# Eight places for x in the column loop, and VectorE's product rooms moved to the transform's input

## The chip, the cores and the metric

One core of a Trainium2 chip runs the whole program. The metric is the device time of one execution in microseconds (us); lower is better. The engines are called as in the profile: PE (TensorE, with PEld its weight loads), DVE (VectorE), ACT (ScalarE), POOL (GpSimd) and SP (SyncE, which here only issues DMA transfers).

## What is computed

A long convolution gated by its input, and then a small expert layer on 128 rows of each of four batches. Cut to what matters:

```python
# x, v: (4, 12608, 128); pos_emb: (12608, 64)
h = np.maximum(pos_emb @ w1, 0.0) @ w2 * np.exp(-0.01 * pos)[:, None]
y = irfft(rfft(x * v, n=2 * S) * rfft(h, n=2 * S))[:, :S]
out = x * y                                   # the gated convolution
scores = out @ moe_w_gate                     # one number per row
top = 128 rows of each batch with the highest scores
out[top] += sigmoid(scores[top]) * (np.maximum(out[top] @ moe_w1, 0) @ moe_w2)
```

## The kernel before, in words

After a filter stage (up to about 106 us) the program goes through 4 batches of 32 groups, a group being 4 of the 128 channels. One group per iteration `t` of the main loop (L1079) passes through a pipeline: transfers of x and v (`load_u`, L253) and their product on POOL (`stage_u`, L259), first transform stage on PE (`f_s1`, L436) with ACT's copy into `te` (L438), second stage on PE (`dft`, L278) with ACT's copy into `qs` (L281), butterflies and the product with the filter on DVE (L445, L442, L450, L451, L456, L457), two sums on POOL (L463, L464), and three iterations later the inverse stage on PE (`f_i`, L273) with ACT's copies into `big` (L487, L488). PE takes the matmuls in the order in which the program is written, and so does every other engine.

When the last group of a batch has gone through `f_i`, the column loop (`P1.run`, L618) runs for that batch, before the next iteration of the main loop. It has 32 half blocks `h` of 4 columns; two half blocks make a block, 16 blocks in the order `ORD`. For a half block PE makes 4 columns (L553, L557), DVE multiplies them in place by x (`fin`, L568), DVE or, for some, POOL multiplies the result by the gate's weights into a room of 4 x 128 numbers (`weigh`, L602), and ACT sums the four columns of that room (L612). DVE's rooms are used in turn, four of them (L621); a room comes free when ACT's sums have read it. From `h` = 28 (`NL`) on, other rooms are used and the sums are left for later, but not in the last batch. After the second half block of a block SP stores it (L591) and fetches the x of a block that comes later (`load_a`, L530).

A block's x lies in a place of 8 x 128 numbers, and seven places are used in turn: block number i of the order lies in place i % 7. Five are their own (`xa`), and two (`XE`) lie over buffers that are free during the loop: the first over `qs` and the start of `mt` (DVE's L450 writes `mt`), the second over `ws` and the start of `yz` (DVE's L456 writes `yz`). The first five blocks of a batch are fetched in halves, one half in each of the ten iterations of `LA` (L44, L1140 to L1144); the two in the XE places when the loop starts; the other nine in the loop. When block i has been multiplied, SP is given the store of block i and behind it the fetch of block i + 6 into the place of block i - 1, which waits until the store of block i - 1 has landed. SP works in order, so everything behind that fetch waits with it.

After the loop the next iteration follows, and its first ACT copy into `qs` (L281) waits until the store from the XE place over `qs` has landed. At the start, iterations t = 0 to 2 fill the five places with zeros on ACT (L1097, L1098).

Of the kernel before, what the change touches and what calls it, by code (L numbers as in the profile page):

```python
# [23 lines left out]
NG = 32  # L24
HC = 4 * N1
# [4 lines left out]
HB = 4  # L30
# [10 lines left out]
PJ = (N3 + 1) // 2  # L41
NC, CO = 4, 2
NE = 3
LA = range(32 - 12, 32 - 2)  # L44
NS, ND = 66, 4
NWARM = 8
JB = 9
# [5 lines left out]
DW = (2, 14)  # L53
OFF, _o = {}, 0
for _n, _k, _w in (("te", 2, 2 * HC), ("qs", 2, HC), ("mt", 1, 2 * HC), ("ws", 1, 888), ("yz", 2, 2 * HC), ("sd", 2, 2 * HC),
                   ("ht", NH, 2 * HC), ("xa", NX, 8 * D), ("wx", 2, HB * D), ("cm", 2, 2 * NC * D), ("x", NU, XC), ("", 1, 2), ("v", NV, XC)):
    OFF[_n] = (_o, _k, _w)
    _o += _k * _w
ARENA = _o
XE = [OFF["qs"][0] + k * 12 * D for k in range(2)]  # L60
CE = [o + 8 * D for o in XE]
POS0, HID0 = 0, PJ * N1


# [107 lines left out]
def hyena_moe(ctx, tc, xg, x2, pos, bw, ww, wg, mw1, mw2, fo, fc, c1, gx, cf, ci, wm, tk, out):  # L172
# [18 lines left out]
    def buf(name, k, shape):  # L191
        o, n, w = OFF[name]
        return view(arena, o + (k + (name == "yz")) % n * w, shape)
# [11 lines left out]
        return view(bank2[k], 0, shape)  # L205

    def gap(k, n):
        return bank2[k].rearrange("p (c x) -> p c x", c=2)[:, :, HC:HC + n]

    def c3(a):  # L210
        return a.rearrange("p (c x) -> p c x", c=2)
# [300 lines left out]
    class P1:  # L512
# [10 lines left out]
        def load_a(self, i, a=0, z=8):  # L523
            if i < len(ORD):
                k = ORD[i]
                j0, j1 = blocks[k]
                z = min(z, j1 - j0)
                o = i % (NX + len(XE))
                self.xa[k] = buf("xa", o, [128, 8, D]) if o < NX else view(arena, XE[o - NX], [128, 8, D])
                nc.sync.dma_start(self.xa[k][P0:P0 + PR, a:z], x2[self.b, :, j0 + a:j0 + z])  # L530

        def comb(self):
# [27 lines left out]
        def fin(self, h):  # L560
            ja, n = self.hbs[h]
            blk = ja // 8
            xa = self.xa[blk]
            js = slice(ja % 8, ja % 8 + n)
            end = self.last and h >= len(self.hbs) - 2
            if end:
                self.weigh()
            nc.vector.tensor_tensor(out=xa[:, js], in0=self.s4.pop(h)[:, :n], in1=xa[:, js], op=ALU.mult)  # L568
            if not end:
                self.weigh()  # L570
                far = ja >= JM and h + 1 < len(self.hbs) and h not in DW
                if h >= NL and not self.last:
                    o = OFF["cm"][0] + 2 * NC * D if h < 30 else OFF["wx"][0]
                    wx = view(arena, o + h % 2 * HB * D, [128, HB, D])
                elif far:
                    wx = view(arena, CE[self.pw % 2], [128, HB, D])
                    self.pw += 1
                else:
                    wx = view(arena, self.wx[self.nw % 4], [128, HB, D])
                    self.nw += 1  # L580
                self.mul = xa[:, js], wx[:, :n], ja, n, far, h
                if far:
                    self.weigh()
            else:
                for k in range(n):
                    nc.vector.scalar_tensor_tensor(out=junk, in0=xa[:, ja % 8 + k], scalar=1.0,
                                                   in1=self.wg, op0=ALU.mult, op1=ALU.mult,
                                                   accum_out=self.sc[:, ja + k:ja + k + 1])
            if ja + n == blocks[blk][1]:
                j0, j1 = blocks[blk]  # L590
                nc.sync.dma_start(out[self.b, :, j0:j1], xa[P0:P0 + PR, :j1 - j0])  # L591
                i = ORD.index(blk)
                if i:
                    self.load_a(i - 1 + NX + len(XE))
                if blk in CB:
                    self.comb()

# [20 lines left out]
        def run(self, ex):  # L618
            self.last = ex is not None
            self.ring = (0, 1, 2) if ex else (3, 2, 0, 1)  # L620
            self.wx = [OFF["wx"][0], OFF["wx"][0] + HB * D, OFF["te"][0] + (2 * HC if ex else 0),  # L621
                       OFF["sd"][0] if ex else OFF["ht"][0] + ((self.b + 1) * NG + 2) % NH * 2 * HC]
            self.wg = ps2(1, [128, D], f"wg_{self.b}")
            nc.scalar.copy(out=self.wg, in_=wgb)
            for k in range(len(XE)):
                self.load_a(NX + k)
            for k in range(2):
                self.comb()
            for h in range(len(self.hbs)):
                self.mm(h)  # L630
                self.fin(h)
                if h == 29:
                    stage_u((self.b + 1) * NG + 5)
                if ex:
                    ex.hook(h, self.wg)
            self.weigh()
            if ex:
                self.mask()
# [440 lines left out]
    for t in range(NT + LAG):  # L1079
# [4 lines left out]
        if t < NT:  # L1084
# [8 lines left out]
                te[t + 1] = f_s1(t + 1)  # L1093
            spare[0] = None
            bg.hook("w", 1)
            load_u(t + NU)
            for k in range(2 * t, min(2 * t + 2, NX)):  # L1097
                nc.scalar.activation(out=buf("xa", k, [128, 8 * D]), in_=one.to_broadcast([128, 8 * D]), func=AF.Copy,  # L1098
                                     scale=0.0)
            if t == 2:  # L1100
                nc.scalar.copy(out=negp, in_=c3(negm))
# [99 lines left out]
```

## Time and profile before

| | |
|---|---|
| median of 3 runs | 869.14 us (866.81 to 874.39) |
| the profiled execution's own time | 866.19 us |
| its span in the trace | 864.1 us |
| around the span | 2.1 us |

A profile shows one execution. Busy time is the time in which an engine executes; what matters is which wait ends last in a stretch. In the timeline a row gives start, length, engine, line, operation, output<-input and shape, and in brackets the idle time of the engine just before and what ended it; an x and a number is how many instructions are merged in the row. A row of SP is the issue of a transfer; its landing comes later.

### The profile page before, as it was taken

The page shows a single profiled execution, that of the slowest core. Times are in us where ns is not written, and L with a number is a line of the kernel's source. Part 1 is how long each engine was busy: PE and PEld are TensorE (multiplying, and loading weights), DVE is VectorE, ACT ScalarE, POOL GpSimd, SP SyncE. Part 2 cuts the span into 40 slices and gives each one's busy share as a digit, 9 for nine tenths or more (in the row PEclk, how much of TensorE's full clock was granted, in tenths as well). Part 3 has the DMA queues.
Part 4 walks back from the last instruction along what each step waited for, and adds up shares of the span by engine and source line. Part 5 has one row for each costly group of instructions (what it writes and reads, how often), then busy time and mean ns, then how long its engine had stood idle before and what let it go on. Part 6 is the DMA issues. An engine that isn't in the chain of part 4 may idle for free.

```text
span 864.1 us, 45963 instructions
## 1 busy us (share of the span) xinstructions
PE 829.2 (96%) x19382; PEld 681.9 (79%) x19382; DVE 758.8 (88%) x1514; ACT 626.1 (72%) x2291; POOL 719.4 (83%) x837
## 2 busy tenths in 40 slices
PE   8999999999999999999999999999999999999875
PEld 5766668888889877777898777779997777779864
DVE  7999989999999789999996998999978989997873
ACT  6766575555559879885588898965797989657961
POOL 5799659999999689898997899989978989879610
PEclk9999999999999999999999999999999999999987
DMA  8044587777878967678779777787798767857810
GB/s 254 3 175 175 207 294 223 223 226 238 268 220 270 314 205 225 212 233 257 226 243 305 258 207 216 229 250 248 225 297 279 218 197 233 241 150 221 289 43 7
DMA packets 83134, 190.25 MB, mean 220 GB/s; under 512 B 9683, under 2 KB 46524, under 8 KB 82928
## 3 DMA queue, kind: packets, MB, share of 16 engines
q1 hardware_dynamic: 82672, 186.79, 68.5%
q8 instruction: 152, 2.49, 1.2%
q0 software_dynamic: 256, 0.52, 0.2%
q14 instruction: 54, 0.44, 0.2%
HBM read 147.57 MB, written 39.71 MB: 217 GB/s over the span
## 4 chain that ended last, share of the span: by engine, by line
PE 66%; DVE 15%; DMA 10%; ACT 5%; issue 3%; POOL 0%; SPq 0%; POOLq 0%; DVEq 0%; ACTq 0%
PE c L273 20%; PE c L278 15%; PE a L436 15%; DMA out_dram<-arena 8%; PE c L412 3%; PE a L393 3%; PE c L393 3%; ACT arena L612 2%; DMA arena<-in_x_dram 2%; DVE big L361 2%; DVE arena L450 2%; DVE c L451 2%; PE a L553 2%; PE a L557 1%; PE c L557 1%
## 5 line engine op out<-in xcount | busy, mean ns | idle before, releaser
L273 PE MATMUL c<-ci_sb,arena 128*23 128x128 f32 x8128 | 249.3, 273 | 5.1 <-issue 2.1
L273 PEld LDWEIGHTS c<-ci_sb,arena 128*23 128x23 f32 x8128 | 227.5, 103 | 14.1 <-issue 5.2
L278 PE MATMUL c<-arena,cf_sb 128*32 128x364 f32 x2048 | 183.5, 470 | 5.5 <-ACT arena L438 3.3
L436 PE MATMUL a<-cons,arena 128*32 128x182 f32 (+1 forms) x4096 | 185.6, 318 | 0.6 <-DVE arena L568 0.6
L436 PEld LDWEIGHTS a<-cons,arena 128*32 128x32 f32 (+1 forms) x4096 | 137.7, 110 | 44.3 <-issue 10.7
L487 ACT COPY big<-c 128x800 f32<-128x800 f32 x127 | 103.8, 817 | 80.7 <-PE c L273 80.2
L612 ACT ACTIVATE arena<-arena 128x128 f32<-128x128 f32 x504 | 148.0, 298 | 9.5 <-DVE arena L602 9.4
L463 POOL TENSOR_TENSOR arena<-arena 128x364 f32<-128x364 f32 x127 | 113.8, 896 | 48.1 <-DVE arena L457 42.3
L438 ACT COPY arena<-a 128x364 f32<-128x364 f32 x256 | 119.5, 467 | 42.4 <-PE a L436 37.8
L259 POOL TENSOR_TENSOR arena<-arena 128x508 f32<-128x508 f32 x128 | 139.1, 1087 | 8.6 <-DMA arena<-in_xg_dram 8.5
L450 DVE TENSOR_TENSOR arena<-c,arena 128x728 f32<-128x728 f32 x127 | 116.3, 915 | 3.8
L451 DVE TENSOR_TENSOR c<-c,arena 128x728 f32<-128x728 f32 x127 | 116.1, 914 | 0.0
L464 POOL TENSOR_TENSOR arena<-arena 128x364 f32<-128x364 f32 x127 | 114.3, 900 | 0.0
L278 PEld LDWEIGHTS c<-arena,cf_sb 128*32 128x32 f32 x2048 | 69.4, 110 | 51.3 <-issue 30.5
L612 ACT ACTIVATION_READ_ACCUMULATOR arena<-arena 128x1 f32 x504 | 95.5, 189 | 0.0
L445 DVE TENSOR_TENSOR c<-c,arena 128x364 f32<-128x364 f32 x128 | 69.6, 543 | 22.1 <-ACT arena L281 19.4
L507 POOL TENSOR_TENSOR big<-big,arena 128x224 f32<-128x224 f32 x128 | 74.4, 581 | 10.0
L540 POOL TENSOR_TENSOR arena<-big 128x512 f32<-128x512 f32 x64 | 79.7, 1276 | 0.6 <-PE a L553 0.3
L456 DVE TENSOR_TENSOR arena<-c,arena 128x364 f32<-128x364 f32 x127 | 68.2, 537 | 13.2 <-POOL big L506 0.5
L281 ACT COPY arena<-c 128x364 f32<-128x364 f32 x128 | 59.1, 462 | 24.1 <-DMA out_dram<-arena 7.4
L506 POOL TENSOR_TENSOR big<-big,arena 128x224 f32<-128x224 f32 x128 | 74.5, 582 | 0.0
L442 DVE TENSOR_TENSOR c<-c,arena 128x364 f32<-128x364 f32 x128 | 69.6, 544 | 2.6
(218 smaller groups left out, 1372.4 us busy)
## 6 DMA issues: line engine op xcount, KB each, us to landing
arena<-in_xg_dram SPq DMA_DIRECT2D x256, 254.0 KB, 3.5
arena<-hd SPq DMA_DIRECT2D x128, 364.0 KB, 4.1
out_dram<-arena SPq DMA_DIRECT2D x64, 420.0 KB, 6.0
arena<-in_x_dram SPq DMA_DIRECT2D x44, 420.0 KB, 4.9
hd<-arena SPq DMA_DIRECT2D x32, 364.0 KB, 2.8
arena<-in_x_dram SPq DMA_DIRECT2D x40, 210.0 KB, 4.6
arena<-in_pos_dram SPq DMA_DIRECT2D x16, 182.0 KB, 3.8
arena<-in_moe_w_dram SPq DMA_DIRECT2D x2, 512.0 KB, 4.7
```

The costliest lines, as they stand in the source:

```text
L259: nc.gpsimd.tensor_tensor(out=x, in0=x, in1=v, op=ALU.mult)
L273: nc.tensor.matmul(o[32 * k:32 * k + c.stop - c.start], lhsT=lhsT[:, c], rhs=rhs, start=True, stop=True)
L278: nc.tensor.matmul(pq[w][a:a + 32], lhsT=cf_sb[:, 2 * w + a // NQ, a % NQ:a % NQ + 32], rhs=te[:, a // NQ], start=True, stop=True)
L436: nc.tensor.matmul(tps[s // 2][c, s % 2], lhsT=u[:, s, c], rhs=c1_sb[:, k], start=True, stop=True)
L438: nc.scalar.copy(out=te[:, :, 2 * h:2 * h + 2].rearrange("p e s i -> p s e i"), in_=tps[h])
L450: nc.vector.tensor_tensor(out=mt, in0=uv, in1=ht[:, 0].unsqueeze(1).to_broadcast([128, 2, HC]), op=ALU.mult)
L451: nc.vector.tensor_tensor(out=uv, in0=uv, in1=ht[:, 1].unsqueeze(1).to_broadcast([128, 2, HC]), op=ALU.mult)
L463: eng.tensor_tensor(out=nat(sd[:, 0]), in0=nat(yz[:, 0]), in1=rev(yz[:, 1]), op=ALU.add)
L464: eng.tensor_tensor(out=nat(sd[:, 1]), in0=rev(yz[:, 0]), in1=nat(yz[:, 1]), op=ALU.subtract)
L487: nc.scalar.copy(out=ay[:, t % NG, :NJ + JM, ss], in_=o3[:, :, :NJ + JM].rearrange("p s x -> p x s"))
L540: nc.gpsimd.tensor_tensor(out=cm[:, e].rearrange("p j (g s) -> p j g s", s=4), in0=av[0], in1=av[1], op=op)
L612: nc.scalar.activation(out=x, in_=x, func=AF.Copy, accum_out=self.sc[:, j:j + 1])
```

## The change

The place `wx`, which held two of DVE's four rooms, becomes an eighth place for x; the places are used in the order `wx`, the five `xa`, the two XE (`XP`). Block i lies in place i % 8. Six blocks are fetched in halves before the loop (`LA` has 12 iterations), two when the loop starts, and eight in the loop; behind the store of block i SP now gets the fetch of block i + 7. The four rooms of the first three batches are now one in `te`, one in `ht`, and two over the last two places of the transform's input `x` (10 spare numbers behind them make these two wide enough). One of those two places is what `load_u` fills for the group six iterations on, so that this call is left out of the iteration ahead of the loop and made in the loop at `h` = 28. The last batch has three rooms. ACT fills a sixth place with zeros in iteration 2. The small buffers between the halves of a PSUM pair (`gap`) become one contiguous piece.

```diff
-LA = range(32 - 12, 32 - 2)
+LA = range(32 - 14, 32 - 2)
...
+XP = [OFF["wx"][0], *(OFF["xa"][0] + k * 8 * D for k in range(NX)), *XE]
+NP0 = NX + 1
...
     def gap(k, n):
-        return bank2[k].rearrange("p (c x) -> p c x", c=2)[:, :, HC:HC + n]
+        return bank2[k][:, HC:HC + 2 * n].rearrange("p (c x) -> p c x", c=2)
...
-                o = i % (NX + len(XE))
-                self.xa[k] = buf("xa", o, [128, 8, D]) if o < NX else view(arena, XE[o - NX], [128, 8, D])
+                self.xa[k] = view(arena, XP[i % len(XP)], [128, 8, D])
                 nc.sync.dma_start(self.xa[k][P0:P0 + PR, a:z], x2[self.b, :, j0 + a:j0 + z])
...
-                    wx = view(arena, self.wx[self.nw % 4], [128, HB, D])
+                    wx = self.wx[self.nw % len(self.wx)]
...
                 if i:
-                    self.load_a(i - 1 + NX + len(XE))
+                    self.load_a(i - 1 + len(XP))
...
-            self.wx = [OFF["wx"][0], OFF["wx"][0] + HB * D, OFF["te"][0] + (2 * HC if ex else 0),
-                       OFF["sd"][0] if ex else OFF["ht"][0] + ((self.b + 1) * NG + 2) % NH * 2 * HC]
+            x = OFF["x"][0] + (NU - 2) * XC
+            o = OFF["te"][0], x, x + HB * D, OFF["ht"][0] + ((self.b + 1) * NG + 2) % NH * 2 * HC
+            if ex:
+                o = OFF["te"][0] + 2 * HC, OFF["sd"][0], OFF["sd"][0] + 2 * HC
+            self.wx = [view(arena, k, [128, HB, D]) for k in o]
...
             for k in range(len(XE)):
-                self.load_a(NX + k)
+                self.load_a(NP0 + k)
...
                 self.mm(h)
                 self.fin(h)
+                if h == NL:
+                    load_u((self.b + 1) * NG + 6)
                 if h == 29:
                     stage_u((self.b + 1) * NG + 5)
...
-            load_u(t + NU)
-            for k in range(2 * t, min(2 * t + 2, NX)):
-                nc.scalar.activation(out=buf("xa", k, [128, 8 * D]), in_=one.to_broadcast([128, 8 * D]), func=AF.Copy,
+            if i < 0 or i % NG < NG - 1:
+                load_u(t + NU)
+            for k in range(2 * t, min(2 * t + 2, NP0)):
+                nc.scalar.activation(out=view(arena, XP[k], [128, 8 * D]), in_=one.to_broadcast([128, 8 * D]), func=AF.Copy,
                                      scale=0.0)
```

The first place is SP's order at the end of a column loop of the first three batches. In the rows `out_dram<-arena` is a block's store, `in_x_dram` the fetch of a block's x, `in_xg_dram` the x and v of one group (`load_u`), `hd` the filter of one group. Before:

```order
L530 DMA arena<-in_x_dram 105x1024
L591 DMA out_dram<-arena 105x1024
L530 DMA arena<-in_x_dram 105x1024
L591 DMA out_dram<-arena 105x1024 x6
L253 DMA arena<-in_xg_dram 128x508 x2
L263 DMA arena<-hd 128x728
L253 DMA arena<-in_xg_dram 128x508 x2
```

Now, where the numbers of the lines are a little higher:

```order
L531 DMA arena<-in_x_dram 105x1024
L592 DMA out_dram<-arena 105x1024
L531 DMA arena<-in_x_dram 105x1024
L592 DMA out_dram<-arena 105x1024 x5
L255 DMA arena<-in_xg_dram 128x508 x2
L592 DMA out_dram<-arena 105x1024 x2
L255 DMA arena<-in_xg_dram 128x508 x2
L265 DMA arena<-hd 128x728
```

One fetch fewer stands in the loop, so seven stores instead of six follow the last fetch, and the x and v of one group now stand ahead of the last two stores.

The second place is ACT's order in iterations 1 and 2, where the copies into `te` (`a` to `arena`) and `qs` (`c` to `arena`) stand with the zero fills. Before:

```order
L1098 ACTIVATE arena<-cons 128x1024 x2
L281 COPY arena<-c_73 128x364
L438 COPY arena<-a_70 128x2x2x91
L438 COPY arena<-a_71 128x2x2x91
L1098 ACTIVATE arena<-cons 128x1024
L1101 COPY c_73<-cons 128x2x64
L487 COPY big<-c_74 128x800
```

Now:

```order
L1105 ACTIVATE arena<-cons 128x1024 x2
L283 COPY arena<-c_73 128x364
L440 COPY arena<-a_70 128x2x2x91
L440 COPY arena<-a_71 128x2x2x91
L1105 ACTIVATE arena<-cons 128x1024 x2
L1108 COPY c_73<-cons 128x128
L489 COPY big<-c_74 128x800
```

One zero fill more stands ahead of the copy into `c_73` (the negative mask) in iteration 2.

## Rows read from the trace of the kernel before

**Rows 1.** The page: its first line, and busy us (share of the span) of PE

```profile
span 864.1 us, 45963 instructions
PE 829.2 (96%) x19382; PEld 681.9 (79%) x19382; DVE 758.8 (88%) x1514; ACT 626.1 (72%) x2291; POOL 719.4 (83%) x837
```

**Rows 2.** Waits in the first column loop, 255 to 300 us: total, times, longest

```profile
DVE arena L568 <- DMA arena<-in_x_dram: 3.1, 3, 1.8
...
ACT arena L281 <- DMA out_dram<-arena: 2.4, 1, 2.4
```

**Rows 3.** Timeline of PE after the first column loop

```profile
293.35 0.82 PE L436 MATMUL a<-cons,arena 128*32 128x182 f32 x16 [0.33 <-DVE arena L568]
...
296.12 1.43 PE L278 MATMUL c<-arena,cf_sb 128*32 128x364 f32 x16 [0.20 <-ACT arena L438]
```

**Rows 4.** Timeline of ACT after the first column loop

```profile
294.74 0.46 ACT L281 COPY arena<-c 128x364 f32<-128x364 f32 x1 [2.41 <-DMA out_dram<-arena]
295.09 0.97 ACT L438 COPY arena<-a 128x364 f32<-128x364 f32 x2
```

**Rows 5.** Timeline of SP, end of the first column loop

```profile
282.81 0.34 SPq L530 DMA_DIRECT2D arena<-in_x_dram  x1
...
286.49 0.34 SPq L530 DMA_DIRECT2D arena<-in_x_dram  x1
286.87 7.15 SPq L591 DMA_DIRECT2D out_dram<-arena  x6
```

**Rows 6.** The chain that ended last, there: start, us, what

```profile
287.78 6.86 DMA out_dram<-arena
```

**Rows 7.** Line L591 in 254 to 300 us: issue to landing

```profile
DMA to landing us min/median/max: 4.7/6.0/6.9
```

**Rows 8.** Timeline of DVE, half blocks 28 and 29

```profile
287.74 1.29 DVE L568 TENSOR_TENSOR arena<-c,arena 128x512 f32<-128x512 f32 x2 [0.25 <-DMA arena<-in_x_dram]
```

**Rows 9.** Timeline of SP, end of the second column loop

```profile
462.20 0.34 SPq L530 DMA_DIRECT2D arena<-in_x_dram  x1
...
464.79 0.34 SPq L530 DMA_DIRECT2D arena<-in_x_dram  x1
465.17 7.90 SPq L591 DMA_DIRECT2D out_dram<-arena  x6
```

**Rows 10.** Timeline of SP, end of the third column loop

```profile
638.49 0.34 SPq L530 DMA_DIRECT2D arena<-in_x_dram  x1
...
641.89 0.34 SPq L530 DMA_DIRECT2D arena<-in_x_dram  x1
642.28 7.48 SPq L591 DMA_DIRECT2D out_dram<-arena  x6
```

**Rows 11.** Timeline of ACT, the copy into qs after the second column loop

```profile
473.48 0.46 ACT L281 COPY arena<-c 128x364 f32<-128x364 f32 x1 [2.06 <-DMA out_dram<-arena]
```

**Rows 12.** The same after the third

```profile
650.73 0.46 ACT L281 COPY arena<-c 128x364 f32<-128x364 f32 x1 [2.94 <-DMA out_dram<-arena]
```

**Rows 13.** Timeline of PE after the second column loop

```profile
468.33 1.95 PE L273 MATMUL c<-ci_sb,arena 128*23 128x128 f32 x64 [0.98 <-DVE arena L568]
...
474.86 1.56 PE L278 MATMUL c<-arena,cf_sb 128*32 128x364 f32 x16 [0.38 <-ACT arena L438]
```

**Rows 14.** Timeline of PE after the third

```profile
652.11 1.43 PE L278 MATMUL c<-arena,cf_sb 128*32 128x364 f32 x16 [0.77 <-ACT arena L438]
```

**Rows 15.** Timeline of ACT, iteration 1: two zero fills

```profile
115.02 2.00 ACT L1098 ACTIVATE arena<-cons 128x1024 f32<-128x1024 f32 x2
```

**Rows 16.** Timeline of DVE, iteration 2

```profile
119.58 0.55 DVE L445 TENSOR_TENSOR c<-c,arena 128x364 f32<-128x364 f32 x1 [1.27 <-ACT c L1101]
```

**Rows 17.** Timeline of DVE, end of the last column loop

```profile
813.75 0.69 DVE L568 TENSOR_TENSOR arena<-a,arena 128x512 f32<-128x512 f32 x1 [0.63 <-DMA arena<-in_x_dram]
...
817.16 0.69 DVE L568 TENSOR_TENSOR arena<-a,arena 128x512 f32<-128x512 f32 x1 [0.88 <-DMA arena<-in_x_dram]
```

**Rows 18.** Timeline of ACT, behind the last sums of the last column loop

```profile
819.28 0.59 ACT L968 ACTIVATE arena<-a 128x512 f32<-128x512 f32 x1
```

More of the change, by code (lines that the diff above doesn't have):

```diff
@@ L55 @@
 for _n, _k, _w in (("te", 2, 2 * HC), ("qs", 2, HC), ("mt", 1, 2 * HC), ("ws", 1, 888), ("yz", 2, 2 * HC), ("sd", 2, 2 * HC),
-                   ("ht", NH, 2 * HC), ("xa", NX, 8 * D), ("wx", 2, HB * D), ("cm", 2, 2 * NC * D), ("x", NU, XC), ("", 1, 2), ("v", NV, XC)):
+                   ("ht", NH, 2 * HC), ("xa", NX, 8 * D), ("wx", 2, HB * D), ("cm", 2, 2 * NC * D), ("x", NU, XC), ("", 1, 10), ("v", NV, XC)):
     OFF[_n] = (_o, _k, _w)
```

## The prediction, made before the changed kernel ran

> **What bounds the kernel now.** I read the page first, then the waits and timelines around the ends of the column loops. The page gives PE 829.2 us of a span of 864.1 us [rows 1]. PE works through nearly everything, so only what leaves PE idle, or DVE in the tail after the last loop, can change the time. The first column loop shows how little that is. The waits name 3.1 us in which DVE waited for a fetch of x, three times, the longest 1.8 us [rows 2]; this is what an eighth place should remove. But PE, whose matmuls run ahead of DVE by the PSUM buffers of the loop, lost only 0.33 us to that, when `f_s1` wanted a bank that DVE had not yet read [rows 3]. The reader should then look at what comes directly behind: ACT's copy into `qs` waited 2.41 us for a store [rows 4], ACT's copies into `te` follow it, and PE's second stage stood until these were done: it started at 296.12 us after an idle time of 0.20 us that ACT ended [rows 3]. So the wait that ends last at the end of a loop is not a fetch. It is the landing of the store from the place over `qs`. The chain of work says the same: its piece is a store issued at 287.78 us that landed 6.86 us later, at 294.64 us [rows 6], and the copy began at 294.74 us [rows 4]. The second and third loops end in the same way, with waits of 2.06 and 2.94 us on ACT [rows 11, 12] and 0.38 and 0.77 us on PE [rows 13, 14].
>
> **The change part by part.**
>
> *The stalls on x.* With seven places the fetch behind the store of block i brings block i + 6, with eight it brings block i + 7. SP's pace stays the same, since each fetch still waits for the store of the block before. The fetch that brings the last block therefore moves up by one step: from 286.49 to 282.81 us in the first loop [rows 5], which is 3.7 us against a longest stall of 1.8 us. I take the stalls as gone in the first three loops. That alone gives back only PE's idle time, 0.33 us in the first loop, 0.98 us in the second [rows 3, 13], and only if nothing behind it is late. The next part says that something is.
>
> *The store that `qs` waits for.* This is the term that decides. Before, block 12 of the order lies in the place over `qs` (12 % 7 = 5, the first XE place); after, it is block 14 (14 % 8 = 6), whose second half block is number 29 of 32. Before, it is the third of the six stores that stand behind the last fetch. After, it is the sixth of seven, and the x and v of one group stand ahead of it too.
>
> In the first loop six stores took SP 7.15 us [rows 5], 1.19 us for one: with the queue full, transfers go at this pace. The copy into `qs` began at 294.74 us, 8.25 us after the last fetch was issued [rows 4, 5]. Three stores stand in that time, 3 x 1.19 = 3.57 us, which leaves a fixed 4.68 us. After the change the last fetch is issued where the one before it is now, at 282.81 us [rows 5]. Behind it come five stores, then x and v, then the store in question. A store has 105 x 1024 numbers and x and v 128 x 508 each, so the two count as 1.21 stores, and the sum is 7.21 x 1.19 = 8.58 us. The copy would begin at 282.81 + 8.58 + 4.68 = 296.07 us, 1.33 us later than before.
>
> Second loop: the pace is 7.90 / 6 = 1.32 us, the copy begins 473.48 - 464.79 = 8.69 us after the last fetch, the fixed part is 8.69 - 3.95 = 4.74 us [rows 9, 11]. After: 462.20 + 7.21 x 1.317 + 4.74 = 476.44 us, 2.96 us later. Third loop: pace 7.48 / 6 = 1.247 us, 650.73 - 641.89 = 8.84 us, fixed part 5.10 us [rows 10, 12]. After: 638.49 + 8.99 + 5.10 = 652.58 us, 1.85 us later. PE already waits at this place in all three [rows 3, 13, 14], so each of these goes through to the end: 1.33 + 2.96 + 1.85 = +6.1 us.
>
> Bounds of this term. Early end: the store cannot be issued before DVE has done half block 29, now at 287.74 + 1.29 = 289.03 us [rows 8]; the stalls ahead of it are 3.1 - 1.8 = 1.3 us [rows 2], so 287.7 us. With the shortest time to landing, 4.7 us [rows 7], it lands at 292.4 us and the copy no longer holds PE. PE then gets back its idle time and no more: 0.33 + 0.20, 0.98 + 0.38 and 0.77 us [rows 3, 13, 14], 2.7 us in all. Late end: issued at 282.81 + 0.38 + 6.21 x 1.19 = 290.6 us and landed after 6.9 us, the longest of the loop [rows 5, 7], it lands at 297.5 us, 2.9 us later than now; three such loops are about +9 us. I take +6.1, which stands on the queue's own pace.
>
> The Trainium skill has a rule for this (DMA: Bandwidth & Descriptors, Queues, rings and completion order): transfers issued by one engine are taken up in order on each DMA engine, but their completion is not first in, first out. By the first half the sum is the one above; by the second half alone the store need not wait for what stands ahead of it, and the sum would be that of the early end. The evenly paced issue of six stores [rows 5] agrees with the first half.
>
> *x and v in the loop.* Counted above as what stands ahead of the store. For themselves they land at about the time of the fifth store, and their product on POOL is asked for one iteration later, with three iterations to go until PE needs it; cost 0, and up to the pace of one transfer if POOL stands. Their call left out ahead of the loop frees the queue there; I take 0.
>
> *DVE's rooms.* Four before and after in three loops: 0. Three instead of four in the last: a bound is one turn of ACT's sums. DVE there waits for the fetches, not for ACT, so 0.
>
> *The earlier half fetches.* Two more of 105 x 512 numbers per batch in the main loop, one fewer whole one in the loop. PE's share of 96% [rows 1] with ten of them says that they hide: 0.
>
> *The sixth fill.* Two fills took ACT 2.00 us, so one is about 1 us [rows 15]. It stands ahead of ACT's copy of the mask, for which DVE already waited 1.27 us in this iteration [rows 16]. DVE is late by the whole of it, at most 1.0 us; DVE is busy for 88% [rows 1], so it takes back some before PE wants its result. Bounds 0 and 1.0, I take +0.6. The contiguous `gap` changes no count and no size: 0.
>
> *The last loop.* Nothing is waiting for `qs` behind it. DVE's two stalls, 0.63 and 0.88 us [rows 17], are on the path to the end, since DVE's last products lead to the top-128 search. ACT's sums finish at 819.28 us whatever the fetches do [rows 18], and that is what is late next. Bounds -1.5 and 0, I take -1.4.
>
> **The sum.** +6.1 + 0.6 - 1.4 = +5.3 us. The profiled execution took 866.19 us, so 871.5 us on its scale. The median of the runs shown is 869.14 us, 2.95 us above that execution; I forecast on the median's scale: 874.4 us.
>
> **The rivals.**
>
> *Faster: the stalls were the price.* The store of block 14 lands early enough, as in the early end above, and all of PE's waits at the three ends go: -2.7 - 1.4 + 0.6 = -3.5 us, 865.6 us. For it speaks that SP is set free 3.7 us earlier [rows 5], so that the stores before it start earlier. Against it: seven transfers stand ahead where two stood. It decides below some five transfers at the pace of 1.19 us. The Trainium skill (Perfetto Trace Analysis, Optimization Strategy) says that a gap that comes back in every turn can mean that SBUF is short of room for the next tile; by that rule another place is the cure and this rival is right. The gaps here do return in every loop, though most of them are DVE's.
>
> *No change.* SP's earlier release and the longer queue cancel, and the copy begins where it began: +0.6 - 1.4 = -0.8 us, 868.3 us.
>
> *Worse than the sum.* The place over `yz` now holds the very last block, stored one pace behind block 14, and DVE's L456 must wait for it. If DVE then comes late by that pace, 1.2 to 1.3 us per loop, and PE with it: +5.3 + 3.7 = +9.0 us, 878.1 us. Against it: DVE comes to L456 only after its four operations behind the copy, which take longer than one pace.
>
> **How the numbers follow.** Chances: the forecast 0.45, faster 0.20, no change 0.20, worse 0.15. Added up from the bounds of all terms the ends are -2.7 - 1.5 + 0 = -4.2 us and +9 + 1.0 + 0 = +10 us, 864.9 and 879.1 us; the range is 865 to 880 us. About 1% is what a measurement of this kernel can tell from no change, 8.7 us here. Faster by more than that needs more than the early ends give, 0.04. Slower by more than that takes the late end or the worst rival, 0.20. Within 1%: 0.76.
>
> **What would show it.** Right: no row of L568 that waits for `in_x_dram` in the first three loops; ACT's L281 behind a loop still waiting for `out_dram`, longer than 2.4 us on the whole, and beginning later from the loop's start by 1 to 3 us; PE's wait for ACT's L438 grown from 0.2 to 0.8 us to 1.5 us and more; in the last loop DVE's end 1.4 us sooner. Wrong: if L281 no longer waits for a store, the faster rival holds; if L568 still waits for fetches, the place did nothing; if L456 waits for `out_dram`, the worst one.

## The result, and the profile after

The changed kernel took 879.95 us (median of 6 runs, 871.97 to 882.9) beside 868.65 us for the kernel before (6 runs): 1.011 times its time, 95% interval 1.006 to 1.016. Run once more beside the last experiments it was 1.0156 times (1.0106 to 1.0205). The forecast was 874.4 us, with a range of 865 to 880 us. The sign and the place were right. The size was about half of what came: +5.3 us was forecast, and +11.3 us came on the medians, +14.4 us on the profiled executions (880.57 and 866.19 us). Slower by more than 1%, which both measurements give (the interval of the first reaches down to 1.006), had a chance of only 0.20.

First the page of the changed kernel: its first line, the busy times, and three of the costliest groups, with busy time, mean ns of one, and idle time before them with what ended most of it. L280 is what was L278, L283 was L281, L261 was L259.

```profile
span 878.8 us, 46043 instructions
PE 831.1 (95%) x19382; PEld 688.2 (78%) x19382; DVE 758.6 (86%) x1514; ACT 627.5 (71%) x2292; POOL 720.1 (82%) x837
...
L280 PE MATMUL c<-arena,cf_sb 128*32 128x364 f32 x2048 | 187.7, 476 | 19.5 <-ACT arena L440 16.5
...
L261 POOL TENSOR_TENSOR arena<-arena 128x508 f32<-128x508 f32 x128 | 139.2, 1087 | 22.6 <-DMA arena<-in_xg_dram 22.6
...
L283 ACT COPY arena<-c 128x364 f32<-128x364 f32 x128 | 59.2, 462 | 40.8 <-DMA out_dram<-arena 20.2
```

The span grew by 14.7 us, PE's busy time by 1.9 us [rows 1]. So most of it is time in which PE stood. 16.5 us of its idle time before the second stage was ended by ACT's copies into `te` (L440), and ACT stood 20.2 us for stores (L283). Those are the two waits that the forecast named.

The waits of the first column loop and what follows it (total us, times, longest):

```profile
ACT arena L283 <- DMA out_dram<-arena: 5.9, 1, 5.9
...
PE c L280 <- ACT arena L440: 4.1, 1, 4.1
...
DVE arena L569 <- PE a L554: 1.4, 2, 0.7
DVE arena L569 <- PE c L554: 1.3, 2, 0.6
```

L569 is the product on DVE (before: L568). In this view it waits for no fetch any more, mostly for PE: the 3.1 us of [rows 2] are gone. The copy into `qs` behind it waits 5.9 us instead of 2.4, and PE 4.1 us instead of 0.2.

The timelines of ACT and of PE behind the first, second and third loop, beside [rows 3, 4] and [rows 11 to 14]:

```profile
298.92 0.46 ACT L283 COPY arena<-c 128x364 f32<-128x364 f32 x1 [5.90 <-DMA out_dram<-arena]
...
481.02 0.46 ACT L283 COPY arena<-c 128x364 f32<-128x364 f32 x1 [5.96 <-DMA out_dram<-arena]
...
665.34 0.46 ACT L283 COPY arena<-c 128x364 f32<-128x364 f32 x1 [8.30 <-DMA out_dram<-arena]
```

```profile
300.16 1.49 PE L280 MATMUL c<-arena,cf_sb 128*32 128x364 f32 x12 [4.09 <-ACT arena L440]
...
482.27 1.44 PE L280 MATMUL c<-arena,cf_sb 128*32 128x364 f32 x8 [4.14 <-ACT arena L440]
...
666.59 1.44 PE L280 MATMUL c<-arena,cf_sb 128*32 128x364 f32 x8 [6.48 <-ACT arena L440]
```

PE's three waits sum to 14.7 us, where they were 0.20, 0.38 and 0.77 us.

PE was also slower behind these waits. The next rows are the stretches from the first of these matmuls (L278, now L280) to the first of L273 (now L275), behind the three loops, before and after. In between lie the same 16 matmuls of the second stage and 32 of the next first stage. A row gives start:end, length, busy time and count of PE, PEld, DVE, ACT and POOL, then PE's granted clock as a share of 2.4 GHz, the share of the DMA engines and GB/s:

```profile
296.12:299.21 3.09, 2.66 (x49) 1.48 (x49) 2.96 (x5) 3.09 (x17) 1.08 (x2) 1.00 0.96 312
474.86:477.95 3.09, 2.79 (x49) 1.79 (x50) 2.96 (x5) 3.09 (x17) 0.58 (x1) 1.00 0.86 285
652.11:655.20 3.09, 2.67 (x49) 1.48 (x50) 2.96 (x5) 3.09 (x17) 0.58 (x1) 1.00 0.90 296
```

```profile
300.16:304.33 4.17, 4.17 (x49) 2.39 (x52) 3.90 (x7) 3.77 (x18) 0.80 (x1) 0.59 0.90 296
482.27:486.14 3.87, 3.87 (x49) 1.87 (x53) 3.63 (x6) 3.67 (x18) 0.51 (x1) 0.63 0.73 246
666.59:670.46 3.87, 3.87 (x49) 1.87 (x53) 3.63 (x6) 3.67 (x18) 0.51 (x1) 0.63 0.60 191
```

Before, PE ran at the higher of its two levels (2.4 GHz) throughout. After it had stood 4.1, 4.1 and 6.5 us, most of the stretch was at the lower one (1.2 GHz), and the same matmuls kept PE busy for 1.5, 1.1 and 1.2 us longer, 3.8 us in all.

SP's queue at the end of the three loops (start, us taken, what), beside [rows 5, 9, 10]:

```profile
284.77 0.34 SPq L531 DMA_DIRECT2D arena<-in_x_dram  x1
285.15 5.60 SPq L592 DMA_DIRECT2D out_dram<-arena  x5
290.85 3.13 SPq L255 DMA_DIRECT2D arena<-in_xg_dram  x2
294.07 1.83 SPq L592 DMA_DIRECT2D out_dram<-arena  x2
...
466.95 0.34 SPq L531 DMA_DIRECT2D arena<-in_x_dram  x1
467.34 5.11 SPq L592 DMA_DIRECT2D out_dram<-arena  x5
472.55 2.98 SPq L255 DMA_DIRECT2D arena<-in_xg_dram  x2
475.65 0.88 SPq L592 DMA_DIRECT2D out_dram<-arena  x2
...
649.48 0.36 SPq L531 DMA_DIRECT2D arena<-in_x_dram  x1
649.89 6.12 SPq L592 DMA_DIRECT2D out_dram<-arena  x5
656.11 2.82 SPq L255 DMA_DIRECT2D arena<-in_xg_dram  x2
659.03 0.96 SPq L592 DMA_DIRECT2D out_dram<-arena  x2
```

The order is the one foretold: the last fetch, five stores, x and v, and then, first of the last two stores, that of block 14, for which the copy into `qs` waits. x and v held SP for 3.2 us in the first loop (290.85 to 294.07 us).

To compare loops that start at different times, I count from the start of DVE's first product in the loop. In the first loop that is, of before and of after:

```profile
255.70 1.28 DVE L568 TENSOR_TENSOR arena<-c,arena 128x512 f32<-128x512 f32 x2
```

```profile
256.44 1.28 DVE L569 TENSOR_TENSOR arena<-c,arena 128x512 f32<-128x512 f32 x2
```

Before, the copy into `qs` starts 294.74 - 255.70 = 39.0 us behind it [rows 4]; after, 298.92 - 256.44 = 42.5 us.

### The profile page after: what moved, and what is told of

Read it like the earlier page. It is cut to its first block, busy times and chain, and to the rows that moved or that the text cites. A ratio compares the mean times of both kernels' runs of the same rounds, so it can differ in the third digit from the quotient of the medians.

```text
span 878.8 us, 46043 instructions
## 1 busy us (share of the span) xinstructions
PE 831.1 (95%) x19382; PEld 688.2 (78%) x19382; DVE 758.6 (86%) x1514; ACT 627.5 (71%) x2292; POOL 720.1 (82%) x837
## 4 chain that ended last, share of the span: by engine, by line
PE 64%; DVE 15%; ACT 12%; issue 3%; DMA 3%; POOL 1%; SPq 1%; POOLq 0%; DVEq 0%; ACTq 0%
PE c L275 19%; PE c L280 15%; PE a L438 15%; ACT arena L613 10%; PE c L414 3%; PE a L395 3%; PE c L395 3%; DVE big L363 2%; DMA out_dram<-arena 2%; DVE arena L452 2%; DVE c L453 2%; PE c L558 1%; DVE c L444 1%; PE a L554 1%; DVE c L447 1%
## 5 line engine op out<-in xcount | busy, mean ns | idle before, releaser
L275 PE MATMUL c<-ci_sb,arena 128*23 128x128 f32 x8128 | 252.4, 273 | 3.2 <-issue 2.1
L275 PEld LDWEIGHTS c<-ci_sb,arena 128*23 128x23 f32 x8128 | 230.0, 103 | 11.1 <-issue 4.5
L280 PE MATMUL c<-arena,cf_sb 128*32 128x364 f32 x2048 | 187.7, 476 | 19.5 <-ACT arena L440 16.5
L438 PE MATMUL a<-cons,arena 128*32 128x182 f32 (+1 forms) x4096 | 187.6, 320 | 0.0
L438 PEld LDWEIGHTS a<-cons,arena 128*32 128x32 f32 (+1 forms) x4096 | 141.2, 111 | 42.7 <-issue 11.9
L261 POOL TENSOR_TENSOR arena<-arena 128x508 f32<-128x508 f32 x128 | 139.2, 1087 | 22.6 <-DMA arena<-in_xg_dram 22.6
L613 ACT ACTIVATE arena<-arena 128x128 f32<-128x128 f32 x504 | 148.0, 298 | 9.4 <-DVE arena L603 9.4
L440 ACT COPY arena<-a 128x364 f32<-128x364 f32 x256 | 118.9, 466 | 39.6 <-PE a L438 28.1
L280 PEld LDWEIGHTS c<-arena,cf_sb 128*32 128x32 f32 x2048 | 73.0, 111 | 64.7 <-issue 29.6
L613 ACT ACTIVATION_READ_ACCUMULATOR arena<-arena 128x1 f32 x504 | 95.5, 189 | 0.0
L283 ACT COPY arena<-c 128x364 f32<-128x364 f32 x128 | 59.2, 462 | 40.8 <-DMA out_dram<-arena 20.2
L458 DVE TENSOR_TENSOR arena<-c,arena 128x364 f32<-128x364 f32 x127 | 68.3, 537 | 12.8
```

What stands on the lines that cost most here:

```text
L261: nc.gpsimd.tensor_tensor(out=x, in0=x, in1=v, op=ALU.mult)
L275: nc.tensor.matmul(o[32 * k:32 * k + c.stop - c.start], lhsT=lhsT[:, c], rhs=rhs, start=True, stop=True)
L280: nc.tensor.matmul(pq[w][a:a + 32], lhsT=cf_sb[:, 2 * w + a // NQ, a % NQ:a % NQ + 32], rhs=te[:, a // NQ], start=True, stop=True)
L438: nc.tensor.matmul(tps[s // 2][c, s % 2], lhsT=u[:, s, c], rhs=c1_sb[:, k], start=True, stop=True)
L440: nc.scalar.copy(out=te[:, :, 2 * h:2 * h + 2].rearrange("p e s i -> p s e i"), in_=tps[h])
L613: nc.scalar.activation(out=x, in_=x, func=AF.Copy, accum_out=self.sc[:, j:j + 1])
```

## The experiments

The theory to be tested: what costs the time is where the store of the `qs` place stands in SP's queue, with x and v ahead of it. The rivals: the late load costs elsewhere (POOL's L261 waits 22.6 us for x and v), the rooms cost, or the eighth place itself does. The table collects what the profiles of all runs show; the runs follow. "Copy" is the start of the copy into `qs`, counted as above, in the three loops; "PE" is the sum of PE's waits for ACT's copies into `te` behind the three loops. The ratio in the last column is the one on record with its interval; it can differ by some tenths of a per cent from the quotient of the medians given further down.

| kernel | copy, us | PE, us | times the kernel before (95%) |
|---|---|---|---|
| before | 39.0, 39.8, 39.9 | 1.35 | 1 |
| changed | 42.5, 42.5, 44.9 | 14.7 | 1.011 (1.006 to 1.016) |
| changed, again | 43.2, 42.4, 41.9 | 12.3 | 1.0156 (1.0106 to 1.0205) |
| load behind the store | 39.5, 41.7, 40.7 | 6.4 | 1.0077 (1.0048 to 1.0107) |
| load ahead, three rooms | 40.2, 41.4, 41.3 | 7.8 | 1.0047 (1.0023 to 1.0071) |
| x, v in one DMA | 42.5, 43.7, 43.3 | 14.6 | 1.0123 (1.0055 to 1.0191) |
| the same, long rows | 42.5, 42.5, 43.2 | 12.6 | 1.0129 (1.0081 to 1.0178) |
| seven places, rooms | 39.1, 41.3, 41.0 | 1.2 | 0.9986 (0.996 to 1.0012) |
| seven places, new order | 38.3, 42.2, 39.4 | 0 | 0.9972 (0.9948 to 0.9997) |
| the same, again | 38.3, 40.0, 38.5 | 0 | 0.9956 (0.9928 to 0.9984) |
| eight places, new order | 37.8, 39.3, 38.6 | 1.2 | 0.9968 (0.9936 to 1.0) |
| both moved | 37.1, 37.9, 37.5 | 0 | 0.9952 (0.9921 to 0.9983) |
| both moved, late fill | 37.4, 39.2, 39.0 | 1.0 | 0.9923 (0.9894 to 0.9952) |
| the same, again | 36.8, 39.0, 37.2 | 0.6 | 0.9935 (0.9904 to 0.9965) |

**x and v behind the store.** The late load moves by one half block:

```diff
-                if h == NL:
+                if h == NL + 1:
                     load_u((self.b + 1) * NG + 6)
```

> One half block later: x and v of the late group are asked for behind the store of block 14 instead of ahead of it; all else is the changed kernel. Theory (SP's time for x and v, about 3.2 us in each of three loops, is what holds that store back): the store is issued about 3.2 us sooner, ACT's copy into qs begins 3 us sooner from each loop's start, PE's waits behind the three loops fall from 4.1, 4.1 and 6.5 us to about 1, 1 and 3.4 us, and the time from 880 to about 871 us. By the forecast's own size (x and v count as 1.21 stores, 1.5 us a loop) it would fall to 875.5 us. Rival (the copy is held by the five whole stores and their landing, not by x and v): stays within 2 us of 880 us. Second rival (POOL's product of x and v comes late): POOL's L261 waits longer and PE with it, 880 us or more.

871.84 us. SP in the first loop, and PE behind all three:

```profile
281.71 0.34 SPq L531 DMA_DIRECT2D arena<-in_x_dram  x1
282.10 7.00 SPq L592 DMA_DIRECT2D out_dram<-arena  x6
289.20 2.38 SPq L255 DMA_DIRECT2D arena<-in_xg_dram  x2
```

```profile
295.39 0.82 PE L280 MATMUL c<-arena,cf_sb 128*32 128x364 f32 x8 [1.13 <-ACT arena L440]
...
475.23 1.12 PE L280 MATMUL c<-arena,cf_sb 128*32 128x364 f32 x12 [3.26 <-ACT arena L440]
...
654.28 1.12 PE L280 MATMUL c<-arena,cf_sb 128*32 128x364 f32 x12 [2.00 <-ACT arena L440]
```

Six stores now leave before x and v, PE's waits fall by 8.3 us, and the median is 8.1 us below that of the changed kernel. The time alone is a weaker witness: the ten runs spread from 868 to 878 us, and the intervals of the two ratios overlap (1.0048 to 1.0107 here). POOL's L261 waits 24.4 us for x and v here, more than in the changed kernel, and the time did not grow, so that wait is not what costs. What speaks against both rivals is the profile and the median together. But the copy comes 3.0, 0.9 and 4.2 us sooner, 2.7 us in the mean, not 3 us in each loop.

**The load ahead of the loop, with three rooms.**

```diff
-            if i < 0 or i % NG < NG - 1:
-                load_u(t + NU)
+            load_u(t + NU)
...
-                if h == NL:
-                    load_u((self.b + 1) * NG + 6)
...
-            x = OFF["x"][0] + (NU - 2) * XC
-            o = OFF["te"][0], x, x + HB * D, OFF["ht"][0] + ...
+            x = OFF["x"][0] + (NU - 1) * XC
+            o = OFF["te"][0], x, OFF["ht"][0] + ...
```

> Eight places in the changed kernel's order, but x and v are asked for ahead of the loop as in the kernel before, and DVE has three rooms instead of four in the first three loops (the two in the x places become one). Theory: with no x and v in the loop the store of block 14 leaves SP about 3.2 us sooner, as in the kernel with the load behind it: 871 us, if three rooms do. Should three rooms not do, DVE's L603 waits for ACT's L613 within the loop and the time is 1 to 3 us higher, 874 us. Rival (x and v have no part in it): 880 us.

871.23 us, as foretold for three rooms that do: DVE's L603 does not wait for L613. With no x and v in the loop at all, the copy still comes 1.4 us later than before (mean of 40.2, 41.4, 41.3 less that of 39.0, 39.8, 39.9). That is the price of the store's rank without x and v.

**Another order of the eight places.** The two places over the transform's tiles come fifth and sixth instead of seventh and eighth, so block 12 lies over `qs`:

```diff
-XP = [OFF["wx"][0], *(OFF["xa"][0] + k * 8 * D for k in range(NX)), *XE]
+XF = [OFF["wx"][0], *(OFF["xa"][0] + k * 8 * D for k in range(NX))]
+XP = XF[:4] + XE + XF[4:]
+PF = [0, 1, 2, 3, 6, 7]
...
-                self.load_a(NP0 + k)
+                self.load_a(4 + k)
...
-            ph[b].load_a(k, e * HB, (e + 1) * HB)
+            ph[b].load_a(PF[k], e * HB, (e + 1) * HB)
```

> The same eight places in another order: the two that lie over the transform's tiles come fifth and sixth, so that block 12 (not 14) is stored from the place over qs and block 13 from the one over yz; the late load stays where it is. Theory (which block lies over qs decides): that store is the fourth behind the last fetch, ahead of x and v, and leaves SP 5 to 6 us sooner than in the changed kernel; ACT's copy into qs no longer waits for it, or under 1 us, PE's waits of 4.1, 4.1 and 6.5 us go, and the time falls to 866 us, at most 869 us. Rival (the longer time comes from the late load or the rooms wherever the store stands): 875 us or more. A cost it may bring: the places over the transform's tiles are fetched at the loop's start and wanted two half blocks sooner, about 8 us after; a fetch takes 4 to 5 us, so 0.

864.51 us, beside 867.97 for the kernel before. The rank decides: with eight places, four rooms and the late load where it was, the time goes from 1.1% above the kernel before to that of the kernel before or just below it (the interval ends at 1.0). The copy still waits for the store, 1.2, 2.8 and 2.0 us, where under 1 us was expected, but PE waits only 1.2 us in all.

**Both edits.**

> Both edits at once: the places in the new order and x and v behind the store of block 14. Theory: with block 12 over qs the store that is waited for is ahead of x and v in any case, so the second edit adds nothing: within 1 us of the kernel with the new order alone, 866 us. Rival (x and v slow the landing of what was issued shortly before them): 1 to 3 us less than that kernel.

862.42 us, 2 us below the kernel with the new order alone; the intervals overlap, so time alone does not tell the two expectations apart. The profile could speak for the rival: the copy comes 0.7, 1.4 and 1.1 us sooner, though the store is now ahead of x and v in both; but the two profiles of the changed kernel differ by 0.7, 0.1 and 3.0 us here, so this is not shown. The row of ACT behind the first loop:

```profile
294.29 0.46 ACT L285 COPY arena<-c 128x364 f32<-128x364 f32 x1 [0.52 <-DMA out_dram<-arena]
```

The copy waits 0.52 us for the store, and PE no longer waits for it at all.

**Seven places with the new rooms and the late load.**

```diff
-LA = range(32 - 14, 32 - 2)
+LA = range(32 - 12, 32 - 2)
...
-XP = [OFF["wx"][0], *(OFF["xa"][0] + k * 8 * D for k in range(NX)), *XE]
-NP0 = NX + 1
+XP = [*(OFF["xa"][0] + k * 8 * D for k in range(NX)), *XE]
+NP0 = NX
```

> The changed kernel without its eighth place: seven places and five early fills as before, but the rooms in the x places and the late load of x and v stay. Block 12 is then over qs again, third of the six stores behind the last fetch, and x and v come behind block 14's first half, so behind that store. Theory (only what stands ahead of the store over qs counts): ACT's copy into qs begins where it did before, 39 to 40 us from the loop's first product, the stalls on x are back (about 2.5 us a loop of DVE's time), PE waits 0.2 to 1.0 us behind each loop, and the time is that of the kernel before: 868 us, 866 to 870. Rival (the late load and the rooms cost by themselves, POOL's product of x and v above all): 871 us or more.

868.42 us beside 867.91. Rooms and a late load that stands behind the awaited store cost nothing that the time shows; the eighth place, with the rank it gives to the store, is what made the kernel slower.

**The kernel before with its seven places in the new order.** Nothing else of the change is in it:

```diff
+XF = [OFF["xa"][0] + k * 8 * D for k in range(NX)]
+XP = XF[:4] + XE + XF[4:]
+PF = [0, 1, 2, 3, 6]
...
-                o = i % (NX + len(XE))
-                self.xa[k] = buf("xa", o, [128, 8, D]) if o < NX else view(arena, XE[o - NX], [128, 8, D])
+                self.xa[k] = view(arena, XP[i % len(XP)], [128, 8, D])
...
```

> The kernel before, with nothing of the change but another order of its seven places: the two over the transform's tiles come fifth and sixth instead of sixth and seventh, so that block 11 is stored from the place over qs instead of block 12, one pace of 1.2 to 1.3 us sooner. Theory: PE's waits behind the loops (1.35 us in all) go, the stalls on x stay, 866.5 us. If the eighth place has a worth of its own, it is the rest of the way to the kernel with eight places in the new order (862.4 us): 3 to 4 us. Rival (the order alone brings it): 863 us.

865.48 us beside 867.91: PE's waits for ACT behind the loops go, the stalls on x stay, and they can reach PE now: behind the second loop it waits 2.4 us for DVE's product (L276 for L570). Once more, with the changed kernel and the fastest one on one chip:

> The seven places in the new order once more, to size what the eighth place is worth by itself. Theory (the stalls on x reach PE by 1 us a loop once nothing behind them is late): 3 to 4 us more than the kernel with eight places that follows, so about 0.997 times the kernel before. Rival (the order brings nearly all): within 1 us of it.

863.98 us, 0.9956 times the kernel before (0.9928 to 0.9984).

**The sixth fill later,** on top of both edits:

```diff
-            for k in range(2 * t, min(2 * t + 2, NP0)):
+            for k in range(2 * t, min(2 * t + 2, NP0 - 1)) if t < 3 else range(t, NP0) if t == NP0 - 1 else ():
```

> Eight places in the new order, x and v behind the store of block 14, and the sixth fill moved from the third iteration to the sixth. Theory: the iteration that had 5.25 us instead of 4.31 has 4.3 us again, 0.9 us less than the kernel without this edit: 861.5 us, which the time can hardly show and the period of PE's groups can. Rival (ACT is as full in the sixth iteration): the same 0.9 us is lost there.

861.92 us. Once more, on that chip:

> Eight places in the new order, x and v behind the store of block 14, the sixth fill late, once more: 0.992 to 0.995 times the kernel before, 861 to 864 us.

861.32 us, 0.9935 times the kernel before (0.9904 to 0.9965): the fastest kernel of the study. It stands 3.6 and 2.7 us below the seven places in the new order, on one chip each time, though the intervals overlap. So the eighth place may be worth some 3 us once the store is out of the way; this is not shown, since the two kernels also differ in the rooms, the late load and the fill, and eight places in the new order without the later load and fill (0.9968) were not faster than seven (0.9972). As for the fill, the changed kernel has this row in its first iterations:

```profile
124.40 1.43 PE L280 MATMUL c<-arena,cf_sb 128*32 128x364 f32 x16 [0.87 <-DVE arena L459]
```

The kernel with the late fill has no wait there (L282 follows at 125.99 us, with none either):

```profile
124.24 1.96 PE L277 MATMUL c<-ci_sb,arena 128*23 128x128 f32 x64
```

The sixth fill cost 0.87 us in the third iteration, and next to nothing in the sixth.

**Is it the number of DMAs?** In the changed kernel, x and v of the late group by one DMA:

```diff
...
-                    load_u((self.b + 1) * NG + 6)
+                    t = (self.b + 1) * NG + 6
+                    if t < NT:
+                        o, d = OFF["x"][0] + t % NU * XC, 2 * XC + 10
+                        nc.sync.dma_start(arena[:, o:o + 2 * d].rearrange("p (k c) -> p k c", k=2)[:, :, :XC],
+                                          xg[t // NG, :, t % NG].rearrange("p k s n -> p k (s n)"))
```

> The changed kernel with x and v of the late group fetched by one DMA of the same rows instead of two. Theory (what the queue needs goes with the bytes and rows, not with the number of DMAs): the store of block 14 still leaves SP about 3 us after the DMA ahead of it, PE's waits stay at 13 to 15 us in all, 878 to 880 us. Rival (each DMA takes a turn of the queue): SP's time for it falls from 3.2 to about 1.6 us, PE's waits to 10 us, 875 us.

879.47 us. SP at the end of the first loop, and ACT and PE behind it:

```profile
282.98 6.28 SPq L594 DMA_DIRECT2D out_dram<-arena  x5
289.36 1.43 SPq L642 DMA_DIRECT2D arena<-in_xg_dram  x1
290.88 1.73 SPq L594 DMA_DIRECT2D out_dram<-arena  x2
```

```profile
297.34 0.46 ACT L283 COPY arena<-c 128x364 f32<-128x364 f32 x1 [5.88 <-DMA out_dram<-arena]
```

```profile
298.72 2.05 PE L280 MATMUL c<-arena,cf_sb 128*32 128x364 f32 x12 [4.20 <-ACT arena L440]
```

The store of block 14 left SP 1.5 us behind the DMA ahead of it (290.88 - 289.36), half of what it was, as the rival had it; and still the copy came no sooner. From that store's issue to the copy it took 297.34 - 290.88 = 6.5 us, where the changed kernel has 298.92 - 294.07 = 4.9 us. What SP no longer waited, the store waited in the queue. So the number of DMAs is not the price, and SP's time for a DMA is not either. The theory was wrong on one point: SP was held half as long, not 3 us as before.

**Is it the number of rows?** Against the kernel just shown, the two places are put side by side, and the one DMA has 128 rows of 1016 numbers:

```diff
-("x", NU, XC), ("", 1, 10), ("v", NV, XC), ("", 1, 10)
+("x", 2, XC), ("", 1, 10), ("xb", 2, XC), ("v", NV, XC)
...
-            x = OFF["x"][0] + (NU - 2) * XC
+            x = OFF["xb"][0] - 8
...
-                        o, d = OFF["x"][0] + t % NU * XC, 2 * XC + 10
-                        nc.sync.dma_start(arena[:, o:o + 2 * d].rearrange("p (k c) -> p k c", k=2)[:, :, :XC],
-                                          xg[t // NG, :, t % NG].rearrange("p k s n -> p k (s n)"))
+                        o = OFF["xb"][0] + XC
+                        nc.sync.dma_start(arena[:, o:o + 2 * XC], xg[t // NG, :, t % NG].rearrange("p k s n -> p (k s n)"))
```

> As the kernel that fetches x and v of the late group by one DMA, but their two places in SBUF are side by side, so that the DMA has 128 rows of 1016 numbers instead of 256 rows of 508. Same bytes, same place in SP's order. Theory (the number of rows is what made x and v cost 2.6 stores, where their bytes are 1.21): they cost about 1.2 stores, the store of block 14 lands about 1.7 us sooner in each loop, PE's waits behind the loops fall from 14.6 to 10 us in all, 874 to 875 us. Rival (rows have no part in it; a read is slow in this place, or the store waits for something else): PE's waits stay at 13 to 15 us, 878 to 880 us.

878.76 us. SP and PE again:

```profile
285.74 6.16 SPq L596 DMA_DIRECT2D out_dram<-arena  x5
292.01 1.11 SPq L644 DMA_DIRECT2D arena<-in_xg_dram  x1
293.21 2.29 SPq L596 DMA_DIRECT2D out_dram<-arena  x2
```

```profile
301.28 2.44 PE L282 MATMUL c<-arena,cf_sb 128*32 128x364 f32 x16 [4.14 <-ACT arena L442]
```

My theory fell here. PE's waits, 12.6 us, are those of the changed kernel's second run (12.3), which has two DMAs of 128 rows each. Half as many rows bring nothing that can be told.

**The changed kernel again,** beside the seven and the eight places in the new order:

> The changed kernel once more, beside the two that follow on one chip: 1.011 times the kernel before, as measured, 878 us.

879.78 us beside 867.31. PE's waits behind the loops are 12.3 us here and 14.7 us in the first profile, so a difference of 2 us between two profiles at this place means nothing.

## Why the prediction was right in its place and short in its size

**The stalls on x.** Right in the first two loops; the third kept 1.8 us of them, in the profile shown first (in the second profile it is the first loop that keeps 2.0 us). What PE regains by their end is small, as foretold: counted from the loop's first product it comes to its wait 0.5, 1.1 and 0.8 us sooner than before.

**The store that `qs` waits for.** This is the step that was mis-sized. Forecast: the copy comes 1.33, 2.96 and 1.85 us later, +6.1 us. Measured from the loop's first product: 3.4, 2.8 and 5.0 us, +11.2 us in the first profile, beyond the late end of +9, and 4.2, 2.6 and 2.0 us, +8.8 us, in the second. It went through to PE as said: PE's waits grew by 13.4 and 11.0 us. The second loop came out as forecast. Three pieces of the sum did not hold:
- The pace was read from a row that merges six issues [rows 5], and these are not evenly paced. One by one they begin at 286.87, 287.38, 287.78, 290.15, 291.55 and 293.32 us, and the last of them stood for DVE, whose last product of the loop ends at 293.3 us. So 1.19 us is an average and not the queue's own pace, and the row does not tell in which order the queue takes up its transfers. The third store, the sixth, and DVE's last product:

```profile
287.78 2.27 SPq L591 DMA_DIRECT2D out_dram<-arena  x1
...
293.32 0.70 SPq L591 DMA_DIRECT2D out_dram<-arena  x1
```

```profile
292.61 0.68 DVE L568 TENSOR_TENSOR arena<-a,arena 128x512 f32<-128x512 f32 x1
```

- x and v were counted by their bytes as 1.21 stores, 1.5 us a loop. Taking them out of the way, behind the store or ahead of the loop, brought the copy forward by 2.1 us a loop (42.9, the mean of the changed kernel's six loops, less 40.8, the mean of the six of the two experiments; no loop of the one group lies within the other, 41.9 to 44.9 and 39.5 to 41.7 us). The two runs with one DMA speak against the number of DMAs and of rows as the reason; what it is stays open.
- The last fetch was taken to come where the fetch before it stood, 282.81 - 255.70 = 27.1 us behind the loop's first product in the first loop [rows 5]. It came at 284.77 - 256.44 = 28.3 us, and all that stands behind it was late by that. In the third loop it came at 649.48 - 620.46 = 29.0 us where 27.6 were taken; in the second, which came out as forecast, at 28.5 us as taken. The same fetch came at 27.1 us in the experiment with the load behind the store, so an arrival taken from one profile has about 1 us of play. The rank of the store alone then cost 1.4 us a loop, measured with the load ahead, where the forecast without x and v gives 0.5 us (6.1 less 4.5, over three loops).

**The sixth fill.** +0.6 us was forecast, 0.87 us measured, within its bounds.

**The last loop.** -1.4 us was forecast. DVE's 32 products there took 38.3 us from the first to the end of the last, 39.2 us before: -0.9 us. From the first product to the end of the span it is 82.0 us, before 83.5 us: -1.5 us (-1.3 in the second profile), so the size was about right. Of DVE's 1.5 us of stalls 0.6 us went to a new wait, not for ACT's sums, as I thought, but for POOL and its room:

```profile
830.66 0.69 DVE L569 TENSOR_TENSOR arena<-c,arena 128x512 f32<-128x512 f32 x1 [0.63 <-POOL arena L603]
```

**What I put at 0.** The rooms and the late load for itself cost nothing that can be measured: the seven places with the rooms and the late load run at 0.9986 times the kernel before. The earlier half fetches are not in that kernel, which has ten of them as before, and no run takes them alone out of the changed one. That they hide is not shown.

**The clock, which the forecast left out.** It lets a delay of the copy go through to the end at its own length and has no term for PE's clock. Behind each of the three waits the same 48 matmuls kept PE busy 1.5, 1.1 and 1.2 us longer, at a granted clock of 0.59, 0.63 and 0.63 where it had been 1.00 (the rows above). In the kernel with both edits, whose PE has no such wait, the clock is 1.00 there.

**The sum over the first profile.** DVE's first product of the four loops starts 0.7, 4.8, 9.6 and 16.2 us later than before, and the span ends 14.7 us later. So the part ahead of the first loop, with the sixth fill, cost 0.7 us, the three loops and the iterations behind them 4.0, 4.8 and 6.6 us, 15.5 us in all, and the last loop gave back 1.5 us. The 15.5 us are, by the starts of PE's matmuls, +13.4 for the waits, +3.8 for the clock, -2.4 for what PE regains ahead of them, -3.6 for other waits of PE, shortly behind the loops, that the kernel before has and this one has not, and +4.4 in the iterations further on, up to the next loop. The forecast had neither the clock nor the 3.6 us; that the two nearly cancel is luck. The 4.4 us were not tried and stay open: the same stretches differ by -0.8 to +2.1 us per loop from the kernel before in the other profiles, those with seven places among them, so nothing can be read from them about the half fetches.

**The rivals.** The faster one and no change fell with the first profile. The worst one (the place over `yz`) was not what came: L458, which was L456, does not wait for a store; its 878 us were near the result for another reason. The Trainium skill's rule that a gap which returns in every turn can mean SBUF short of room for the next tile (Perfetto Trace Analysis, Optimization Strategy) holds here only on a condition that the runs show: one more place made the kernel 1.1 to 1.6% slower while it put the awaited store further back, and no longer did once that store stood early; the 3 us that it may bring there are not clear of noise.

## What to carry to other kernels

A place more in a ring changes which tile sits in each place, so look first at who waits for the place that is shared with the next stage, and count what stands ahead of that store in its queue; here the order of the places was worth more than their number (1.011 to 0.997 with the same eight). Put loads that nobody awaits soon behind the store that somebody does. Price a transfer in a full queue by the arrival of what stands behind it, not by its bytes and not by how long the issuing engine was held.

## What the runs showed of the hardware that I had not expected

- The time for which SP is held by a DMA is no measure of its cost. One DMA for x and v held SP for 1.1 to 1.4 us, two held it for 2.8 to 3.1 us, and the copy that waits for the store behind them began at 42.5 to 43.7 us and 41.9 to 44.9 us of the loop.
- 508 KB in 256 rows of 2 KB or in 128 rows of 4 KB took 7.0 and 7.2 us from issue to landing, in these two rows of the two pages:

```profile
arena<-in_xg_dram SPq DMA_DIRECT2D x3, 508.0 KB, 7.0
```

```profile
arena<-in_xg_dram SPq DMA_DIRECT2D x3, 508.0 KB, 7.2
```

- Ahead of the store, these bytes cost 2.1 us a loop, where 1.5 us had been put for them by their share of bytes.
- A wait of PE costs more than its length: after it had stood 4.1 to 6.5 us, the same 48 matmuls took 3.9 to 4.2 us of its time instead of 2.7 to 2.8 us, at the lower of its two clock levels for most of the stretch.
